# Moving one more block of w2 to the upper column groups in the closing matmuls of a decode layer

## The chip, the cores and the metric

The kernel runs on 1 core of one Trainium2 chip. The metric is the device time of one execution in microseconds; medians of several executions are quoted. A run's profile starts at the first instruction of the program and spans some 1.8 us less than the measured time. Times below that are given to a nanosecond (79.188 us) are read from the trace's records of single instructions and of semaphore updates, counted from the start of the span. Each trace is one execution.

The engines are named as in the profile: PE multiplies matrices and PEld loads its weights, DVE is the vector engine, ACT the scalar engine, and SyncE (SP, with its queue SPq) issues the transfers. The granted clock is the share of full speed that PE was allowed. ffn1 and ffn2 are the first and the second matrix product of the feed-forward part.

Ratios are the mean time of one kernel's fast runs over that of the other's fast runs of the same rounds, so they are not quite the ratios of the medians quoted beside them.

## The reference

One decode step of an adaptive layer: a modulation from `c`, windowed attention over a key and value cache, and a ReLU feed-forward part. The argument is about the last lines:

```python
mod = (_silu(c) @ w_mod).reshape(c.shape[0], 6, 1, -1)
sa, ca, ga, sb, cb, gb = ...
...
h = _layernorm(x) * (1 + cb) + sb
x = x + gb * (relu(h @ w1) @ w2)      # batch 4, 512 -> 1792 -> 512
```

w1 and w2 are 1792 KB each; with the cache window, wq, wo and w_mod the kernel reads 32 MB.

## The kernel before

One queue streams every weight in a fixed order; w1 and w2 come last, w2 in five pieces. A block is 128 of the 1792 hidden features, so w2 has 14 blocks (`FT` = 14).

```python
nc.sync.dma_start(out=w1_sb, in_=B_w1.rearrange("(p t) n -> p t n", t=DT))
W2_CHUNKS = [(0, 4), (4, 4), (8, 3), (11, 2), (13, 1)]      # first block, number of blocks
for (m0, e) in W2_CHUNKS:
    nc.sync.dma_start(out=w2_dst[:, m0 * D:(m0 + e) * D],
                      in_=B_w2[m0 * P:(m0 + e) * P, :].rearrange("(q e) n -> q (e n)", e=e))
```

The second matrix product uses 32 columns of the array per matmul. Four such column groups exist. A block in the lower groups (0 and 1) sums into `z_ps`, one in the upper groups (2 and 3) into `za_ps`; a block is four matmuls, two steps (`x`) of two groups (`g`). "Lone" below means that only two of the four groups work in a step.

```python
def closing(parts):
    for x in range(NX):                       # NX = 2
        for (ps, q, j, src, rhs, start, stop, cols) in parts:
            for g in range(2):
                q0 = (q + g) * CG             # CG = 32
                nc.tensor.matmul(out=ps[q0:q0 + CG, cols], lhsT=rows(src, j, x), rhs=rhs(2 * x + g),
                                 start=start and x == 0, stop=stop and x == NX - 1, tile_position=(0, q0))
...
ZUP = (0, 1, 2, 3, 6, 7)
ZLOW = tuple(m for m in range(FT) if m not in ZUP)
...
def zpart(m):
    mine = ZUP if m in ZUP else ZLOW
    return (za_ps if m in ZUP else z_ps, 2 if m in ZUP else 0, m, uT32, lambda j: w2_sb[:, m, j * DH2:(j + 1) * DH2],
            m == mine[0], m == mine[-1], slice(None))

for (m0, m1) in [(0, 8), (8, FT)]:
    ffn1(m0, m1)
for ms in [(0,), (1,), (2, 4), (3, 5), (6,), (7,)]:
    closing([zpart(m) for m in ms])
zc = work.tile([2 * CG, DH2], f32, name="zc")
nc.scalar.copy(out=zc[:], in_=za_ps[2 * CG:P, :])                       # ACT
nc.vector.tensor_tensor(out=zc[:], in0=zc[:], in1=gb2[:], op=ALU.mult)  # DVE
nc.vector.tensor_tensor(out=zc[:], in0=zc[:], in1=x12_ps[:], op=ALU.add)
for m in range(8, FT):
    closing([zpart(m)])
zg = work.tile([2 * CG, DH2], f32, name="zg")
nc.vector.tensor_tensor(out=zg[:], in0=z_ps[:], in1=gb2[:], op=ALU.mult)
res = work.tile([2 * CG, DH2], bf16, name="res")
nc.vector.tensor_tensor(out=res[:], in0=zg[:], in1=zc[:], op=ALU.add)
... # two DMAs store res
```

Of the kernel before, what the change touches and what calls it, by code (L numbers as in the profile page):

```python
# [17 lines left out]
def kernel(  # L18
# [23 lines left out]
    FT = Dff // P  # L42
# [146 lines left out]
    def closing(parts):  # L189
        for x in range(NX):  # L190
            for (ps, q, j, src, rhs, start, stop, cols) in parts:
                for g in range(2):
                    q0 = (q + g) * CG
                    nc.tensor.matmul(out=ps[q0:q0 + CG, cols], lhsT=rows(src, j, x), rhs=rhs(2 * x + g),  # L194
                                     start=start and x == 0, stop=stop and x == NX - 1, tile_position=(0, q0))
# [272 lines left out]
        return w1_sb[:, t, m0 * P + m - m0:(m0 + e) * P:e]  # L468


    ZUP = (0, 1, 2, 3, 6, 7)
    ZLOW = tuple(m for m in range(FT) if m not in ZUP)
    z_ps = psA.tile([2 * CG, DH2], f32, tag="t", name="z_ps")
    za_ps = psA.tile([P, DH2], f32, tag="t", name="za_ps")

    def ffn1(m0, m1):
        u_ps = psA.tile([P, m1 - m0, 2, B], f32, tag="t", name=f"u_ps_{m0}")
        for m in range(m0, m1):
            for t in range(DT):
                nc.tensor.matmul(out=u_ps[:, m - m0].rearrange("p s b -> p (s b)"), lhsT=w1_cols(t, m),  # L480
                                 rhs=ab[:, t].rearrange("p s b -> p (s b)"), start=(t == 0), stop=(t == DT - 1))
        us = work.tile([P, m1 - m0, B], f32, name=f"us_{m0}")
        nc.vector.tensor_tensor(out=us[:], in0=u_ps[:, :, 0, :], in1=rstd2[:].unsqueeze(1).to_broadcast([P, m1 - m0, B]),
                                op=ALU.mult)
        nc.vector.tensor_tensor(out=us[:], in0=us[:], in1=u_ps[:, :, 1, :], op=ALU.add)
        nc.vector.tensor_scalar_max(out=put(uT32[:, m0:m1, :]), in0=us[:], scalar1=0.0)
# [5 lines that stand above are left out]

    for (m0, m1) in [(0, 8), (8, FT)]:
        ffn1(m0, m1)
    for ms in [(0,), (1,), (2, 4), (3, 5), (6,), (7,)]:
        closing([zpart(m) for m in ms])
    zc = work.tile([2 * CG, DH2], f32, name="zc")
    nc.scalar.copy(out=zc[:], in_=za_ps[2 * CG:P, :])
    nc.vector.tensor_tensor(out=zc[:], in0=zc[:], in1=gb2[:], op=ALU.mult)
    nc.vector.tensor_tensor(out=zc[:], in0=zc[:], in1=x12_ps[:], op=ALU.add)  # L500
    for m in range(8, FT):
        closing([zpart(m)])

    zg = work.tile([2 * CG, DH2], f32, name="zg")
# [36 lines left out]
```

## Time and profile before

| | before |
|---|---|
| median of 3 runs (range) | 85.43 us (85.37 to 85.53) |
| span of the profile | 83.66 us |
| last landing of w1 | 75.70 us |
| last landing of w2 blocks 8-10 / 11-12 / 13 | 79.188 / 79.828 / 80.152 us |
| first matmul of block 8 / 11 | 79.229 / 79.869 us |
| DVE starts zg | 80.731 us |

A landing is the last of the increments that a transfer gives its semaphore. The lines of the profile behind the table, and how they are read, stand in the prediction.

### The profile page before, as it was taken

How to read it: one execution, taken by the hardware profiler on the slowest of the kernel's cores; microseconds unless marked ns; L12 is line 12 of the kernel's file. 1: busy time of each engine (PE TensorE's matmuls, PEld its weight loads, DVE VectorE, ACT ScalarE, POOL GpSimd, SP SyncE). 2: the span in 40 equal slices, each digit the busy share in tenths (PEclk: the TensorE clock that was granted, in tenths of full speed). 3: DMA queues.
4: the chain of work that ended last, by engine and by line, in shares of the span. 5: the costliest groups of instructions: out<-in, count | busy, mean ns of one | idle time of the engine just before them, and what ended most of it. 6: DMA issues, size and time to landing. Idle time of an engine off the chain costs nothing.

```text
span 83.7 us, 2373 instructions
## 1 busy us (share of the span) xinstructions
PE 56.1 (67%) x1064; PEld 47.0 (56%) x1064; DVE 26.5 (32%) x76; ACT 23.8 (28%) x38; POOL 6.0 (7%) x21
## 2 busy tenths in 40 slices
PE   0001006999953989999999905999555779577950
PEld 0000006995852964988777504999555248567740
DVE  0201300367043010375546668650003120251350
ACT  3201001664302000697777819611000010001000
POOL 5894000000000000000000000000000000000000
PEclk9999999999985555799999998589555555555555
DMA  2899999998999999999999999999999999999600
GB/s 31 306 466 423 407 427 423 529 501 360 392 380 423 419 423 415 415 427 419 415 419 423 423 415 419 419 427 419 415 415 431 407 415 436 426 388 403 251 8 2
DMA packets 4257, 32.14 MB, mean 384 GB/s; under 512 B 528, under 2 KB 664, under 8 KB 1304
## 3 DMA queue, kind: packets, MB, share of 16 engines
q1 hardware_dynamic: 4192, 31.99, 92.2%
q8 instruction: 8, 0.13, 0.6%
q10 hardware_dynamic: 24, 0.01, 0.0%
q0 software_dynamic: 32, 0.00, 0.0%
q14 instruction: 1, 0.01, 0.0%
HBM read 31.99 MB, written 0.00 MB: 382 GB/s over the span
## 4 chain that ended last, share of the span: by engine, by line
DMA 63%; PE 27%; DVE 4%; issue 1%; SPq 1%; ACT 1%; DVEq 0%
DMA w<-in_B_w_dram 26%; DMA v<-in_A_v_cache_dram 24%; DMA k<-in_A_k_cache_dram 14%; PE ktp L225 9%; PE qT_ps L322 4%; PE sc_ps L237 2%; PE z_ps L194 2%; PE mT L273 2%; PE mT L275 2%; PE u_ps L480 1%; PE za_ps L194 1%; PE m_ps L259 1%; PE m_ps L262 1%; PE st_ps_var L289 1%; PE gb_ps L194 1%
## 5 line engine op out<-in xcount | busy, mean ns | idle before, releaser
L225 PE MATMUL ktp<-ident_k,k 128*128 128x128 bf16 x256 | 18.2, 240 | 5.6 <-DMA k<-in_A_k_cache_dram 5.6
L225 PEld LDWEIGHTS <-k 128*128 128x128 bf16 x256 | 17.2, 110 | 8.2 <-DMA k<-in_A_k_cache_dram 5.7
L230 ACT COPY kT<-ktp 128x1024 bf16<-128x1024 bf16 x16 | 15.5, 1015 | 17.4 <-PE ktp L225 16.3
L228 DVE COPY kT<-ktp 128x1024 bf16<-128x1024 bf16 x16 | 11.1, 692 | 16.2 <-PE ktp L225 15.9
L360 PE MATMUL oT_ps<-pT,v 128*128 128x16 bf16 x256 | 7.1, 172 | 1.9 <-issue 1.9
L360 PEld LDWEIGHTS <-v 128*128 128x128 bf16 x256 | 7.1, 100 | 2.0 <-issue 2.0
L237 PE MATMUL sc_ps<-kT,qpad 128*32 128x512 bf16 x64 | 5.6, 445 | 0.4 <-DVE qpad L326 0.4
L377 PE MATMUL pT_ps<-ident_bf,p_rep 128*128 128x128 bf16 x32 | 3.3, 291 | 2.9 <-DVE p_rep L371 2.9
L200 PE MATMUL tp<-ident_bf,cx_sb 8*128 8x8 bf16 x4 | 0.3, 174 | 7.3 <-POOL xs L180 7.3
L377 PEld LDWEIGHTS <-p_rep 128*128 128x128 bf16 x32 | 2.9, 135 | 3.4 <-DVE p_rep L371 3.4
L322 PE MATMUL qT_ps<-hT,wq_sb 128*128 128x4 bf16 x128 | 3.6, 166 | 1.4 <-DVE ab L315 1.4
L322 PEld LDWEIGHTS <-wq_sb 128*128 128x128 bf16 x128 | 3.5, 104 | 1.5 <-DMA wq_sb<-in_A_wq_dram 1.5
L200 PEld LDWEIGHTS <-cx_sb 8*128 8x128 bf16 x4 | 0.2, 114 | 7.3 <-DMA cx_sb<-in_A_x_dram 7.3
L429 ACT COPY y<-y_ps 128x256 f32<-128x256 f32 x1 | 0.4, 372 | 9.6 <-DVE y L428 9.6
L424 PE MATMUL y_ps<-wo_sb,o 128*32 128x512 bf16 x16 | 2.1, 619 | 1.0 <-DVE o L415 0.9
L436 PEld LDWEIGHTS <-wo_sb 128*128 128x128 bf16 x64 | 2.5, 120 | 0.6 <-DMA wo_sb<-in_A_wo_dram 0.6
L402 DVE TENSOR_TENSOR oT_sb<-oT_ps,rb 128x128 bf16<-128x128 f32 x1 | 0.3, 291 | 7.8 <-PE oT_ps L360 7.8
L436 PE MATMUL y_ps<-o,wo_sb 128*128 128x4 bf16 x64 | 2.4, 173 | 0.5 <-DMA wo_sb<-in_A_wo_dram 0.5
L371 DVE TENSOR_TENSOR p_rep<-e_sb,mi 128x512 int32<-128x512 int32 x4 | 2.5, 686 | 0.7 <-ACT e_sb L366 0.7
L194 PEld LDWEIGHTS <-uT 128*32 128x32 bf16 x56 | 2.3, 135 | 0.6 <-issue 0.2
L432 PEld LDWEIGHTS y_ps<-sel_b,y 128*128 128x128 f32 x8 | 1.8, 327 | 1.4 <-DVE y L428 1.4
L237 PEld LDWEIGHTS <-qpad 128*32 128x32 bf16 x64 | 1.3, 103 | 2.2 <-DVE qpad L326 0.7
(113 smaller groups left out, 56.2 us busy)
## 6 DMA issues: line engine op xcount, KB each, us to landing
k<-in_A_k_cache_dram SPq DMA_DIRECT2D x8, 1024.0 KB, 28.4
v<-in_A_v_cache_dram SPq DMA_DIRECT2D x8, 1024.0 KB, 19.8
wq_sb<-in_A_wq_dram SPq DMA_DIRECT2D x1, 4096.0 KB, 23.6
wo_sb<-in_A_wo_dram SPq DMA_DIRECT2D x4, 1024.0 KB, 19.9
wmod_sb<-in_w_mod_dram SPq DMA_DIRECT2D x1, 2304.0 KB, 9.5
w<-in_B_w_dram SPq DMA_DIRECT2D x1, 1792.0 KB
w<-in_B_w_dram SPq DMA_DIRECT2D x2, 512.0 KB, 19.9
wmod_sb<-in_w_mod_dram SPq DMA_DIRECT2D x1, 768.0 KB, 4.4
```

Of the source, the lines that this page charges most:

```text
L194: nc.tensor.matmul(out=ps[q0:q0 + CG, cols], lhsT=rows(src, j, x), rhs=rhs(2 * x + g), start=start and x == 0, stop=stop and x == NX - 1, ...
L225: nc.tensor.transpose(out=tp[:, ii, :], in_=k_tiles[gi][:, iq * IQ + ii, :], identity=ident_k)
L228: nc.vector.tensor_copy(out=dst, in_=tp[:])
L230: nc.scalar.copy(out=dst, in_=tp[:])
L237: nc.tensor.matmul(out=sc_ps[hw * CG:(hw + 1) * CG, half * HALF:(half + 1) * HALF], lhsT=qpad[:, b, par, hw, :], rhs=kT[:, half * (NI // 2 ...
L322: nc.tensor.matmul(out=qT_v[:, hq, :], lhsT=wq_sb[:, t, hq * Dh:(hq + 1) * Dh], rhs=hT[:, t, :], start=(t == 0 and hq == 0), stop=(t == DT ...
L360: nc.tensor.matmul(out=oT_ps[:, hw, par].rearrange("p b r -> p (b r)"), lhsT=v_tiles[h][:, i, :], rhs=pT[:, i, c0:c0 + B * rep], start=(fi ...
L371: nc.vector.tensor_tensor(out=p_w[:, ws, :], in0=e_w[:, ws].unsqueeze(2).to_broadcast([P, WQ // 2, B]), in1=mi4[:].unsqueeze(1).to_broadca ...
L377: nc.tensor.transpose(out=tp[:, ii, :], in_=p_rep[:, i // 2, :, i % 2], identity=ident_bf[:])
L424: nc.tensor.matmul(out=y4_ps[q0:q0 + CG, :], lhsT=o4[:, l, g % 2, g // 2, :], rhs=wo_sb[:, g, l, :], start=(g == 0 and l < 4), stop=(g == ...
L432: nc.tensor.matmul(out=y_ps[:, t, :], lhsT=y4[:, t, :], rhs=sel_b[:], start=(t == 0), stop=False)
L436: nc.tensor.matmul(out=y_ps[:, m, :], lhsT=wo_sb[:, g, l, m::DT], rhs=o4[:, l, g % 2, g // 2, 0:B], start=False, stop=(g == NP - 1 and l = ...
```

## The change

Its intent is to shorten the run of lone steps at the end: block 8 goes to the upper groups and is issued beside block 9, so that the four matmuls of a step work in four column groups.

```diff
-    ZUP = (0, 1, 2, 3, 6, 7)
+    ZUP = (0, 1, 2, 3, 6, 7, 8)
...
-    for ms in [(0,), (1,), (2, 4), (3, 5), (6,), (7,)]:
+    for ms in [(0,), (1,), (2, 4), (3, 5), (6,), (7,), (8, 9)]:
         closing([zpart(m) for m in ms])
...
-    for m in range(8, FT):
+    for m in range(10, FT):
         closing([zpart(m)])
```

## The prediction

> **What bounds the kernel now.** I started with the page, to see which resource is busy where. Its DMA rows, and the table of transfers by size, are:
>
> ```profile
> DMA  2899999998999999999999999999999999999600
> GB/s 31 306 466 423 407 427 423 529 501 360 392 380 423 419 423 415 415 427 419 415 419 423 423 415 419 419 427 419 415 415 431 407 415 436 426 388 403 251 8 2
> ...
> w<-in_B_w_dram SPq DMA_DIRECT2D x1, 384.0 KB, 17.7
> ...
> w<-in_B_w_dram SPq DMA_DIRECT2D x1, 256.0 KB, 15.9
> w<-in_B_w_dram SPq DMA_DIRECT2D x1, 128.0 KB, 13.7
> ```
>
> One slice is 83.7/40 = 2.09 us. From slice 2 to slice 37 (to 77.4 us) the 16 DMA engines are nine tenths busy at 400 to 430 GB/s, and slice 38 (77.4 to 79.5 us) still moves 251 GB/s. So the stream of weights reaches into the stage that the change touches: w2 comes in five pieces, and the three lines are its last three: blocks 8 to 10 (384 KB), 11 and 12 (256 KB), 13 (128 KB). The last number is the time from issue to landing. The issues stand in the SyncE rows of the timeline; each line is the answer for its own short window, in the order of the pieces:
>
> ```profile
> 61.46 0.33 SPq L129 DMA_DIRECT2D w<-in_B_w_dram  x1
> ...
> 63.95 0.33 SPq L129 DMA_DIRECT2D w<-in_B_w_dram  x1
> ...
> 66.44 0.33 SPq L129 DMA_DIRECT2D w<-in_B_w_dram  x1
> ```
>
> The sums give the landings: 61.46 + 17.7 = 79.16, 63.95 + 15.9 = 79.85, 66.44 + 13.7 = 80.14 us. The trace's records of the semaphore updates have them finer: blocks 8 to 10 at 79.188, 11 and 12 at 79.828, 13 at 80.152 us; blocks 4 to 7 at 78.258.
>
> Next I read the chain that ended last, because it should name what sets the end:
>
> ```profile
> 53.99 21.72 DMA w<-in_B_w_dram
> ...
> 78.91 0.34 PE za_ps L194 x8
> 79.25 1.46 PE z_ps L194 x24
> 80.71 0.02 issue
> 80.73 0.29 DVE zg L505
> ```
>
> Taken alone it says that 24 lone z_ps matmuls (blocks 8 to 13, four each) stand on the path for 1.46 us, and that DMA left the path when w1 landed at 75.70. I don't believe the second part. The timeline of the tail shows why:
>
> ```profile
> 78.62 0.64 PE L194 MATMUL za_ps<-w,uT 128*32 128x128 bf16 x8
> 79.23 1.46 PE L194 MATMUL z_ps<-w,uT 128*32 128x128 bf16 x24
> 79.23 1.19 PEld L194 LDWEIGHTS <-uT 128*32 128x32 bf16 x23 [0.25 <-issue]
> 79.29 0.26 ACT L498 COPY zc<-za_ps 64x128 f32<-64x128 f32 x1 [3.58 <-PE za_ps L194]
> 79.59 0.28 DVE L499 TENSOR_TENSOR zc<-zc,gb 64x128 f32<-64x128 f32 x1 [1.29 <-ACT zc L498]
> 79.91 0.28 DVE L500 TENSOR_TENSOR zc<-zc,x_ps 64x128 f32<-64x128 f32 x1
> 80.73 0.28 DVE L505 TENSOR_TENSOR zg<-z_ps,gb 64x128 f32<-64x128 f32 x1 [0.55 <-PE z_ps L194]
> ```
>
> The weight loads are idle for 0.25 us before 79.23, put down to "issue", that is, to nothing the profile could name. Matmul by matmul, the starts in the trace fill this in. A pair of block 7 starts at 78.937 and 78.938; the next could follow 0.107 us later, at 79.045, yet block 8 starts at 79.229. That is 0.041 us after its piece of w2 landed (79.188). Block 11 starts at 79.869, again 0.041 us after its piece (79.828). Block 4 starts at 78.302, 0.044 us after its piece (78.258), although there a free slot falls on the same moment. So PE follows the stream of w2 with almost no work in hand, and the chain view misses these waits. Blocks 8 to 10 end their last slot at 79.739 + 0.107 = 79.846, only 0.023 us before block 11 can start. From 79.869 on, three blocks run back to back (last start 80.379, end 80.693), and zg follows at 80.731.
>
> **What the Trainium skill says.** "TensorE: Matmul & The Clock Gate", section Back-to-back issue gap, gives N/1.2 ns per matmul at the cold clock, 106.7 ns for N = 128. The trace agrees: the granted clock in the tail is 0.50 and starts in one column group are 106 to 107 ns apart. The same page, Part 3: Packing small matmuls, says that matmuls in different column tiles run concurrently; in the paired steps of blocks 2, 4 and 3, 5 the four matmuls of a step start within 0.021 us, and steps follow every 0.107 us, as they do for two matmuls alone. Perfetto Trace Analysis, Roofline, puts a single core's ceiling at some 435 GB/s over 16 DMA engines; the rows above run at 400 to 430. "DMA: Bandwidth & Descriptors", section Why a DMA increments its semaphore by 16 and not by 1, says that only the full count means the data has landed. I therefore took the last of the increments as each piece's landing, and the 0.041 us starts agree.
>
> **The change, part by part.** No instruction is added or removed: 56 matmuls, 56 weight loads, and the same ACT and DVE operations. Block 8's four matmuls move from z_ps (column groups 0 and 1) to za_ps (groups 2 and 3), and are issued interleaved with block 9's.
>
> On PE: blocks 8 and 9 one after the other take 4 steps, together 2. The saving is 2 steps x 0.107 = 0.214 us of PE time. Where it falls: the pair needs the piece of blocks 8 to 10, as block 8 does now, so it starts at 79.229 again. Before, six steps filled 79.229 to 79.846 (0.617 us). Four steps end at 79.846 - 0.214 = 79.632 us. Block 11 still needs its piece, landed at 79.828, and starts at 79.869. PE's wait before it grows from 0.023 to 79.869 - 79.632 = 0.237 us. Blocks 11 to 13 are unchanged, so the last z_ps matmul ends at 80.693 and zg starts at 80.731, as now. Gain at the end: 0.
>
> On ACT and DVE: the sum in za_ps is now complete with block 8 instead of block 7. Its last matmul is that of the pair's second step. In the first paired step of before, z_ps starts at 78.302 and the second step's za_ps at 78.405, so 0.103 us later: 79.229 + 0.103 = 79.332, and with 0.314 us duration the end is 79.646 us (before 78.938 + 0.314 = 79.252). The ACT copy followed by 0.041 us: 79.687. The copy's start to the end of the second zc operation took 79.907 + 0.279 - 79.293 = 0.893 us before. So zc is ready at about 80.58 us, and DVE can take zg 0.035 us later, at 80.615. It needs it at 80.731. The slack shrinks from 80.731 - (80.186 + 0.035) = 0.510 us to 0.116 us, and stays positive: cost 0.
>
> DMA: nothing in the diff changes an issue or what an issue waits for. Sum: 0.00 us, so 85.43 stays 85.43; I round to 85.4.
>
> **Rivals.** First, the change works as intended, and the time falls by the whole 0.214 us to 85.43 - 0.21 = 85.2. For it: the chain view shows z_ps matmuls on the path and no DMA after 75.70. Against it: the two starts, each 0.041 us after a landing, with 0.640 us between the landings and 0.640 between the starts. It would need the 256 KB piece to land some 0.2 us nearer to the 384 KB one, and the stream's rate leaves no room: 256 KB (262,144 bytes) in 0.640 us is 410 GB/s, the rate of the whole stream.
>
> Second, the later za_ps makes zc the last to arrive, and DVE takes zg late. The slack of 0.116 us would have to be overdrawn, by a slower copy or by one more wait on PE. If za_ps came another 0.2 us late, zg would start 0.08 us late and the time would be 85.5. For it: the slack left is less than half a DVE operation (0.283 us), and the copy and the two zc operations now hang on block 8's late piece. Against it: each term of the 0.116 us comes from a row of the same trace, and all three operations keep their size.
>
> Third, a mixture: PE's idle 0.2 us could move the granted clock. The clock is 0.50 throughout the tail already, after stretches at full speed, and the idle time is short; I give it nothing.
>
> **Range and chances.** Every mechanism lies between -0.21 and +0.1 us, that is -0.25% to +0.1%. The three runs of before spread by 0.16 us, and another chip or build may shift the median by as much again. I take 85.15 to 85.7 as the range for 8 in 10. Two per cent are 1.7 us, eight times the largest effect that I can name: faster 0.01, same 0.98, slower 0.01.
>
> **What would show it right or wrong.** Right: the first z_ps and za_ps matmuls of blocks 8 and 9 start together at the landing of the 384 KB piece plus 0.04 us; block 10 ends 0.2 us or more before the 256 KB piece lands; block 11 starts 0.04 us after that landing, with PE idle before it; the copy of za_ps starts near 79.69 instead of 79.29; DVE's idle time before zg shrinks from 0.55 to about 0.15 us, still ended by z_ps. Wrong: block 11 starts as soon as block 10 has ended, earlier than now relative to the end of the stream (first rival), or zg follows zc within 0.04 us (second rival). A larger move would mean that w2's landings themselves moved, which no line of the diff explains.

## The result

The changed kernel takes 85.50 us (median of 6 runs, 85.36 to 85.72), the kernel before in the same rounds 85.43 us (85.37 to 85.67). The ratio is 1.0005, with a 95% interval of 0.9987 to 1.0023: the same. A gain of the whole 0.214 us of the prediction's first rival would be a ratio of 0.9975, which lies outside the interval.

These are the three last pieces of w2 in the DMA view of the changed kernel (size, median time from issue to landing):

```profile
w<-in_B_w_dram SPq DMA_DIRECT2D x1, 384.0 KB, 17.9
...
w<-in_B_w_dram SPq DMA_DIRECT2D x1, 256.0 KB, 16.0
w<-in_B_w_dram SPq DMA_DIRECT2D x1, 128.0 KB, 13.9
```

They are issued at 61.49, 63.98 and 66.45 us. Issues and times to landing are those of before to within 0.2 us, so the transfers were not touched. Now the timeline of its tail (start, duration, engine, line, operation, tiles, count, idle time and what ended it):

```profile
79.40 0.29 PE L194 MATMUL z_ps<-w,uT 128*32 128x128 bf16 x2
79.45 0.34 PE L194 MATMUL za_ps<-w,uT 128*32 128x128 bf16 x2
79.48 1.38 PE L194 MATMUL z_ps<-w,uT 128*32 128x128 bf16 x18
79.82 0.26 ACT L498 COPY zc<-za_ps 64x128 f32<-64x128 f32 x1 [3.94 <-PE za_ps L194]
80.03 0.55 PEld L194 LDWEIGHTS <-uT 128*32 128x32 bf16 x11 [0.19 <-issue]
80.12 0.28 DVE L499 TENSOR_TENSOR zc<-zc,gb 64x128 f32<-64x128 f32 x1 [1.67 <-ACT zc L498]
80.44 0.28 DVE L500 TENSOR_TENSOR zc<-zc,x_ps 64x128 f32<-64x128 f32 x1
80.89 0.28 DVE L505 TENSOR_TENSOR zg<-z_ps,gb 64x128 f32<-64x128 f32 x1 [0.17 <-PE z_ps L194]
```

The reader should look at three rows. The za_ps and z_ps rows at 79.40 to 79.48 are blocks 8 and 9, which now run side by side. The weight loads (PEld) are idle for 0.19 us before 80.03, "issue" again: that is block 11, and the idle time was not there before. And DVE's idle time before zg is 0.17 us where it was 0.55, still ended by z_ps.

The chain that ended last (start, duration) shows the same place:

```profile
54.05 21.82 DMA w<-in_B_w_dram
...
79.79 0.22 PE z_ps L194 x5
80.01 0.02 issue
80.03 0.84 PE z_ps L194 x12
...
80.89 0.29 DVE zg L505
```

In its terms nothing is amiss: records of PE run to 80.01, and 0.02 us of "issue" follow. It names neither landing, because a matmul's record lasts 0.31 us and covers the gap.

Single starts and landings give the account to the nanosecond. The last three pieces of w2 landed 0.160 to 0.166 us later in this profile than in that of before (w1 too, 75.87 against 75.70; in unpaired_a below, which has the same transfers, the last piece lands at 80.150 as before), so the last column takes 0.160 off.

| us | before | changed | difference, less 0.160 |
|---|---|---|---|
| blocks 8-10 landed | 79.188 | 79.348 | 0 |
| first matmul of block 8 | 79.229 | 79.391 | 0.002 |
| last step of block 10 starts | 79.739 | 79.693 | -0.206 |
| blocks 11-12 landed | 79.828 | 79.988 | 0 |
| first matmul of block 11 | 79.869 | 80.030 | 0.001 |
| ACT copy of za_ps starts | 79.293 | 79.824 | 0.371 |
| second zc operation starts | 79.907 | 80.438 | 0.371 |
| zg starts | 80.731 | 80.892 | 0.001 |

The two steps are saved on PE (-0.206 us). PE then stands still: block 10's last step occupies its groups until 79.693 + 0.107 = 79.800, and block 11 starts at 80.030, so the wait is 0.230 us where it was 0.023.

### The profile page after: what moved, and what is told of

The parts are those of the page before. It is cut to its first block, busy times and chain, and to the rows that moved or that the text cites. A ratio compares the mean times of both kernels' runs of the same rounds, so it can differ in the third digit from the quotient of the medians.

```text
span 83.8 us, 2373 instructions
## 1 busy us (share of the span) xinstructions
PE 56.8 (68%) x1064; PEld 47.3 (56%) x1064; DVE 26.5 (32%) x76; ACT 23.9 (28%) x38; POOL 5.9 (7%) x21
## 4 chain that ended last, share of the span: by engine, by line
DMA 78%; PE 14%; SPq 2%; DVE 2%; issue 1%; DVEq 0%
DMA wq_sb<-in_A_wq_dram 28%; DMA w<-in_B_w_dram 26%; DMA v<-in_A_v_cache_dram 23%; PE qT_ps L322 4%; PE sc_ps L237 2%; PE ktp L225 2%; PE za_ps L194 2%; PE z_ps L194 2%; SPq L83 2%; PE u_ps L480 1%; SPq L93 0%; SPq L92 0%; DVE zg L505 0%; DVE res L507 0%; DVE qpad L326 0%
## 5 line engine op out<-in xcount | busy, mean ns | idle before, releaser
L225 PE MATMUL ktp<-ident_k,k 128*128 128x128 bf16 x256 | 18.7, 243 | 5.6 <-DMA k<-in_A_k_cache_dram 5.6
L377 PE MATMUL pT_ps<-ident_bf,p_rep 128*128 128x128 bf16 x32 | 2.8, 244 | 2.9 <-DVE p_rep L371 2.9
L377 PEld LDWEIGHTS <-p_rep 128*128 128x128 bf16 x32 | 2.1, 109 | 3.6 <-DVE p_rep L371 3.5
```

The source lines that it names most:

```text
L225: nc.tensor.transpose(out=tp[:, ii, :], in_=k_tiles[gi][:, iq * IQ + ii, :], identity=ident_k)
L377: nc.tensor.transpose(out=tp[:, ii, :], in_=p_rep[:, i // 2, :, i % 2], identity=ident_bf[:])
```

## The experiments

The theory: PE waits for the pieces of w2, and this wait swallows the saved steps (landing theory). The main rivals: the gap before block 8 is something else; pairing saves nothing; zc has become the last. Twelve kernels were run in three sessions: noland_b, noland_a, merge_b and merge_a; then, on another chip, the fills and up12; then the rest. The kernel before took 85.68, 85.60 and 85.65 us in them (medians of 11 runs each). Since profiles differ by up to 0.4 us in when the stream ends, the traces are compared from a landing, or from the first ffn2 matmul, to zg.

**noland_b and noland_a: blocks 8 to 13 of w2 are not read.** Both give wrong results, the first from the kernel before, the second from the changed one. All pieces are still loaded, and blocks 4 to 7 still wait for theirs.

```diff
-  lambda j: w2_sb[:, m, j * DH2:(j + 1) * DH2]
+  lambda j: w2_sb[:, m % 8, j * DH2:(j + 1) * DH2]
```

> The kernel before, but the matmuls of blocks 8 to 13 multiply by blocks 0 to 5 of w2, which landed early (wrong result on purpose); all pieces are still loaded. Landing theory (PE waits for the pieces of w2, and that hid the change): block 8 follows block 7 without the gap, 0.107 us after it, all twelve lone steps run back to back, and zg starts 0.155 us earlier relative to the first ffn2 matmul, ratio about 0.998. Rival (the gap before block 8 is something else, such as a fixed cost of turning to the other accumulator): the gap of 0.18 us stays and the ratio is 1.000.

> The changed kernel with the same edit (wrong result on purpose). Landing theory: with the waits gone the two saved steps count, z_ps is complete 0.214 us sooner than in noland_b; but zc, ready about 0.07 us later than that, becomes the last, so zg starts about 0.145 us sooner than in noland_b and 0.30 us sooner than in the kernel before: ratio about 0.9965, and DVE takes zg 0.035 us after zc. Rival (a paired step costs as much as two lone ones): no difference from noland_b.

noland_b: 85.11 us, ratio 0.9936 (0.9915 to 0.9956). noland_a: 85.30 us, ratio 0.9957 (0.9938 to 0.9975). The gap before block 8 is gone, so it was the landing. But the size is off: zg starts 2.441 us after the first ffn2 matmul instead of 2.944, that is 0.50 us sooner and not 0.155. The timeline of noland_b tells why:

```profile
78.88 0.32 PE L194 MATMUL za_ps<-w,uT 128*32 128x128 bf16 x2
78.96 0.32 PE L194 MATMUL z_ps<-w,uT 128*32 128x128 bf16 x2
78.98 0.32 PE L194 MATMUL za_ps<-w,uT 128*32 128x128 bf16 x2
...
79.20 0.32 PE L194 MATMUL za_ps<-w,uT 128*32 128x128 bf16 x2
79.28 1.17 PE L194 MATMUL z_ps<-w,uT 128*32 128x128 bf16 x18
...
80.49 0.28 DVE L505 TENSOR_TENSOR zg<-z_ps,gb 64x128 f32<-64x128 f32 x1
```

Before the z_ps row at 78.96, z_ps had eight matmuls, those of blocks 4 and 5; so this row is block 8. It starts while za_ps has the second step of block 6 and both steps of block 7 still to come (78.98 to 79.20), although these six matmuls stand ahead of it in the program, whose order on every engine is that of the kernel before. Here PE let a matmul go whose column groups were free; how far ahead it can reach was not measured. So steps of the lower and the upper groups need not be issued side by side to run so, and "lone" steps add up only where a landing holds them. Only the landing of blocks 4 to 7 at 78.511 still holds z_ps: it starts at 78.554 and runs without a break to its last start at 80.134, 16 steps, one every 0.105 us.

noland_a was to be 0.145 us sooner than noland_b and is 0.10 us later (2.540 us from the first ffn2 matmul to zg); the means of the timed runs, 85.31 and 85.13, go the same way. Its timeline:

```profile
79.39 0.74 PE L194 MATMUL z_ps<-w,uT 128*32 128x128 bf16 x10
...
80.27 0.28 DVE L500 TENSOR_TENSOR zc<-zc,x_ps 64x128 f32<-64x128 f32 x1
80.48 0.27 DVE L505 TENSOR_TENSOR zg<-z_ps,gb 64x128 f32<-64x128 f32 x1
```

The z_ps row ends at 80.13 (its last step starts at 79.823), yet zg starts at 80.476, 0.206 us after the second zc operation and with no wait of its own: it queued behind zc. Hence:

**nozc_a: noland_a with less work on zc.**

```diff
-    nc.vector.tensor_tensor(out=zc[:], in0=zc[:], in1=gb2[:], op=ALU.mult)
```

> noland_a without the multiplication of zc by gb2 (wrong on purpose), so zc is ready 0.32 us sooner. If zc was what held noland_a back, zg now follows z_ps: about 2.24 us after the first ffn2 matmul instead of 2.54, ratio to the kernel before about 0.992, and the change's two steps show at last: 0.2 us less than noland_b's 2.44. Rival (something else on PE holds noland_a): zg stays at 2.5 us.

85.04 us, ratio 0.9929 (0.9907 to 0.9951). Its output is wrong, which doesn't matter for the time. From the first ffn2 matmul to zg it takes 2.240 us, as expected, 0.201 us less than noland_b.

```profile
79.55 0.74 PE L194 MATMUL z_ps<-w,uT 128*32 128x128 bf16 x10
...
80.33 0.28 DVE L504 TENSOR_TENSOR zg<-z_ps,gb 64x128 f32<-64x128 f32 x1
```

z_ps ends at 80.29 and zg follows 0.04 us later. Counted from the landing of blocks 4 to 7, which z_ps waits for in both kernels, zg comes after 1.764 us here and 1.978 in noland_b: 0.214 us less. So the two steps are worth 0.2 us, and in the changed kernel two things in a row stand before them: the landings, and zc behind those. The timed ratios of nozc_a and noland_b, from different sessions, are too close to show it; the traces do.

**merge_b and merge_a: one landing instead of two.** The same bytes, correct results. `W2_CHUNKS` also sets the stride at which ffn1 reads the columns of w1 (`w1_cols`): its matmuls for blocks 8 to 12 start 0.040 us apart instead of 0.026 to 0.030. That does not reach the end, since `uT` is complete at 78.65 us in merge_b and 78.89 in merge_a, long before the merged piece lands (79.887 and 80.124).

```diff
-    W2_CHUNKS = [(0, 4), (4, 4), (8, 3), (11, 2), (13, 1)]
+    W2_CHUNKS = [(0, 4), (4, 4), (8, 5), (13, 1)]
```

> The kernel before with blocks 8 to 12 of w2 in one piece of 640 KB instead of 384 and 256. Landing theory: block 8 now starts 0.04 us after the merged piece lands, near where block 11 started, and twelve steps in a row follow: zg 0.64 us later, ratio about 1.0075. Rival (landings do not set the tail): ratio 1.000.

> The changed kernel with the same merged piece. Landing theory: no landing falls after the pair any more, so the saved steps count up to where zc takes over: zg 0.12 us sooner than in merge_b, 0.52 us later than in the kernel before, ratio about 1.006, zg 0.035 us after zc. Rival (pairing saves nothing): the same as merge_b.

merge_b: 86.16 us, ratio 1.0064 (1.0041 to 1.0088). merge_a: 86.06 us, ratio 1.0046 (1.0026 to 1.0065). In merge_b the wait is long enough for the profile to name it:

```profile
79.93 1.46 PE L194 MATMUL z_ps<-w,uT 128*32 128x128 bf16 x24 [0.55 <-DMA w<-in_B_w_dram]
```

It is the wait before the same block 8 that the profile of before called "issue". After it twelve steps run in a row, and zg comes 1.543 us after the merged landing. In merge_a it is 1.345 us: the pair gains 0.198 us once no later landing stands behind it. The means of the timed runs, 86.22 and 86.07, agree in sign and size, though their intervals overlap. I had expected a gain of 0.12 us only, with zc taking over:

```profile
80.17 0.29 PE L194 MATMUL za_ps<-w,uT 128*32 128x128 bf16 x2 [0.54 <-DMA w<-in_B_w_dram]
...
81.21 0.28 DVE L500 TENSOR_TENSOR zc<-zc,x_ps 64x128 f32<-64x128 f32 x1
81.47 0.28 DVE L505 TENSOR_TENSOR zg<-z_ps,gb 64x128 f32<-64x128 f32 x1
```

zg does not read zc; only res does. DVE starts it as early as 0.206 us after the second zc operation started (noland_a), not 0.28 + 0.035 us. In merge_a that allows 81.212 + 0.206 = 81.418, and z_ps was the later one.

**after_fill2, before_fill2 and after_fill8: filling the hole.** Lone steps into a tile that nobody reads (`fill_ps`, of the size of `z_ps`), between blocks 10 and 11; n is 1 or 4, each turn being two steps. Results are correct.

```diff
     for m in range(10, FT):      # range(8, FT) in before_fill2
         closing([zpart(m)])
+        if m == 10:
+            for i in range(n):
+                closing([(fill_ps, 0, 9, uT32, lambda j: w2_sb[:, 9, j * DH2:(j + 1) * DH2], i == 0, i == n - 1, slice(None))])
```

> The changed kernel plus two lone steps (four matmuls of block 9 into a PSUM tile that nobody reads) between blocks 10 and 11. Landing theory: they fit the hole of 0.23 us before block 11; ratio to the kernel before 1.000, block 11 still 0.04 us after its piece. Rival (PE steps set the end): 0.21 us more, ratio 1.0025.

> The kernel before plus the same two lone steps in the same place. Landing theory: there is no hole there (0.023 us), so block 11 starts 0.19 us late and the end moves by as much, ratio 1.0022. Rival (PE time is free throughout the tail): 1.000.

> The changed kernel plus eight lone steps in the same place. Landing theory: 8 x 0.107 - 0.23 = 0.62 us late, ratio 1.0073. Rival (PE steps set the end already): 0.86 us, 1.010.

after_fill2: 85.71 us, ratio 1.0017 (1.0000 to 1.0033). before_fill2: 85.79 us, ratio 1.0023 (1.0004 to 1.0043). after_fill8: 86.17 us, ratio 1.0065 (1.0053 to 1.0078), which leaves the rival's 1.010 out. The two small fills cannot be told apart by their times. The trace of after_fill2 can be read:

```profile
79.82 0.43 PE L194 MATMUL fill_ps<-w,uT 128*32 128x128 bf16 x4
...
80.06 0.82 PE L194 MATMUL z_ps<-w,uT 128*32 128x128 bf16 x12
```

The fill's last step starts at 79.929 and the piece lands at 80.017; block 11 starts 0.042 us after that, and zg 0.905 us after it, where the kernel before has 0.903 and the changed one 0.904. The hole was free. With eight steps it is 1.554 us, that is 0.65 us more, against an expected 0.62. before_fill2 is a poor witness: in its profile the granted clock rose from 0.50 to 1.00 at 80.67 us, within the last steps, so zg came only 0.952 us after the landing; block 11, though, started at 80.285, 0.211 us after the landing instead of 0.041.

**up12: the late zc priced.** Block 12 instead of block 8 in the upper groups of the kernel before; correct result.

```diff
-    ZUP = (0, 1, 2, 3, 6, 7)
+    ZUP = (0, 1, 2, 3, 6, 7, 12)
-    for ms in [(0,), (1,), (2, 4), (3, 5), (6,), (7,)]:
+    for ms in [(0,), (1,), (2, 4), (3, 5), (6,), (7,), (8,), (9,), (10,), (11, 12)]:
...
-    for m in range(8, FT):
+    for m in range(13, FT):
```

> The kernel before with block 12, not block 8, moved to the upper groups and issued beside block 11; za_ps is then complete 0.64 us after the landing of blocks 8 to 10. This prices the late zc: z_ps could end 0.1 us sooner than before, but zc follows za_ps by 0.93 us, so zg starts 0.035 us after zc, about 0.52 us later than in the kernel before: ratio about 1.006. Rival (zc is hidden whatever za_ps does): 0.999 to 1.000.

86.05 us, ratio 1.0053 (1.0040 to 1.0066):

```profile
81.27 0.28 DVE L500 TENSOR_TENSOR zc<-zc,x_ps 64x128 f32<-64x128 f32 x1
81.47 0.28 DVE L505 TENSOR_TENSOR zg<-z_ps,gb 64x128 f32<-64x128 f32 x1
```

zc sets the end here: zg starts 1.311 us after the landing of blocks 11 and 12, 0.41 us later than in the kernel before (expected 0.52; the 0.11 too much is again the DVE overlap). The second rival of the prediction is real, then, only not in reach of the change.

**unpaired_a: the other column groups alone, without the issue side by side.**

```diff
-    for ms in [..., (6,), (7,), (8, 9)]:
+    for ms in [..., (6,), (7,), (8,), (9,)]:
```

> One part of the change alone: block 8 in the upper groups, but issued before block 9 and not interleaved with it. The runs without landings suggest that PE starts a matmul whose column group is free although an earlier one of another group still waits for its group. If so, block 9 starts within 0.02 us of block 8 as in the changed kernel, zg comes 0.90 us after the 256 KB piece landed, ratio 1.000. Rival (strict order): block 9 starts about 0.2 us after block 8; the end still doesn't move, since the hole before block 11 covers it.

85.51 us, ratio 0.9990 (0.9970 to 1.0010). The weight loads of block 8 begin when its piece has landed (79.181), and z_ps of block 9 follows at once:

```profile
79.22 0.46 PEld L194 LDWEIGHTS <-uT 128*32 128x32 bf16 x12 [0.16 <-issue]
79.24 0.29 PE L194 MATMUL z_ps<-w,uT 128*32 128x128 bf16 x2
79.28 0.34 PE L194 MATMUL za_ps<-w,uT 128*32 128x128 bf16 x2
```

Block 9 starts 0.013 us after block 8 (79.236 against 79.223), and zg 0.904 us after the 256 KB landing. The interleaved issue does nothing that PE does not do by itself.

**fine_b and fine_a: finer last pieces.** The runs above say that the only thing left to gain here is the work behind the last landing. Same bytes, correct results.

```diff
-    W2_CHUNKS = [(0, 4), (4, 4), (8, 3), (11, 2), (13, 1)]
+    W2_CHUNKS = [(0, 4), (4, 4), (8, 2), (10, 2), (12, 1), (13, 1)]
```

> The kernel before with finer last pieces of w2: blocks 8-9, 10-11, 12, 13 instead of 8-10, 11-12, 13; the same bytes. Landing theory: after the last landing only block 13 is left, so zg comes 0.48 us after it instead of 0.58: 0.10 us sooner, ratio 0.999 if the smaller pieces do not slow the stream. Rival (the smaller pieces cost more than that): ratio over 1.000.

> The changed kernel with the same finer pieces. Landing theory: PE has caught up before the last landing in either kernel, so it equals fine_b: zg 0.48 us after the last landing, ratio 0.999. Rival (the two saved steps add to it): 0.21 us below fine_b.

fine_b: 85.92 us, ratio 1.0035 (1.0008 to 1.0063). fine_a: 85.91 us, ratio 1.0031 (1.0006 to 1.0056). Up to zg both do what the theory says: 0.479 us after the last landing in either, against 0.579 in the kernel before. Nevertheless they are slower.

zg and the first store, at 80.65 and 81.28, are 0.08 us earlier than in the kernel before (80.73 and 81.36), and the second store has landed at 82.667 instead of 82.749. From there to the end of the span it takes 1.121 us instead of 0.908. At its end, SyncE waits for the semaphores of all transfers in a fixed order. In the kernel before the stores use the last two of them (numbers 117 and 118). One more transfer shifts the rotation: a store now uses number 107, which stands second in the order, so SyncE waits there until 82.69 and only then goes through the remaining four waits, some 0.06 us each. This accounts for the span of this profile (0.213 - 0.082 = 0.131 us longer: 83.788 against 83.657). It was not tested by itself, but merge_b and merge_a fit it: with one transfer fewer, their stores use numbers 116 and 117, one wait stands behind them, and the stretch is 0.967 and 0.956 us. The timed means of fine_b and the kernel before differ by more, 0.30 us (interval 0.07 to 0.54); the profiled execution was the fastest of the six. Whether the smaller pieces also slow the stream, as the rival has it, stays open. A version with finer last pieces but the old number of transfers, such as blocks 0-5, 6-9, 10-11, 12, 13, was not run. No kernel of this study with correct results beats both.

## Why the prediction was right

It gave 85.4 us, a range of 85.15 to 85.7 and 0.98 for "same"; 85.50 us came.

- **What bounds the tail.** PE waits for the landings of w2. Shown: the gap before block 8 vanishes when blocks 8 to 13 are not read, and where the wait is longer (merge_b) the profile itself puts it down to the transfer.
- **PE saves 0.214 us and waits as much longer before block 11.** Measured 0.206 saved, and a wait of 0.230 instead of the predicted 0.237 us. That this wait is free time is shown by after_fill2 (from landing to zg 0.905 us) and after_fill8.
- **zc stays hidden.** The copy was predicted 0.394 us later than before (79.687) and came 0.371 later. The slack before zg was sized as 0.116 us; by the same rule it is 80.892 - (80.718 + 0.035) = 0.139. The rule itself was too strict: zg need not wait for the end of the second zc operation, so the slack is 80.892 - (80.438 + 0.206) = 0.248 us. That is a term mis-sized on the safe side.
- **First rival, 0.214 us of gain.** Its size was right and its place wrong. It appears where no landing stands behind the pair: 0.198 us in merge_a against merge_b, 0.201 in nozc_a against noland_b.
- **Second rival, zc last.** It did not happen in the changed kernel; it does in up12 and noland_a.
- **Third rival.** The granted clock was 0.50 throughout the tail of the changed kernel too.
- **A loose reading.** The prediction puts the stream at 400 to 430 GB/s from slice 2 to 37, but its own row has 306 to 529 up to slice 12 (and 388 to 436 after it). With each packet's bytes spread over its duration, every stretch of 2 us between 4 and 76 us moves 411 to 434 GB/s, so what follows from it stands.

One sentence of the working holds only by circumstance: that blocks 8 and 9 "one after the other take 4 steps". They do because the landing comes after block 7 has ended. Without it PE runs block 8 beside blocks 6 and 7 unasked, and so my expectations for noland_b and noland_a missed, the second even in sign.

## What to carry to other kernels

Where a stream of weights ends inside the last stage, compare each group's first start with the landing of what it reads before counting instructions; work saved ahead of a landing is only a longer wait. The chain of waits can hide such a landing when matmul records are longer than the gap. And when a change moves work to a side sum, ask how much later that sum's own chain of operations ends, since it may be the next bound.

## What the Trainium skill lacked or had wrong

- "TensorE: Matmul & The Clock Gate", Part 3: Packing small matmuls, says that matmuls keep program order in start and end. In noland_b block 8's first z_ps matmul starts at 78.956 us, before the second step of block 6 and both steps of block 7 in za_ps (78.982 to 79.196), which precede it in the program; in unpaired_a a matmul of block 9 starts at 79.240, before two of block 8 at 79.284 and 79.306.
- No page that I read tells of the closing waits at the program's end and their order: one more transfer in fine_b made the stretch from the last landing of a store to the end of the span 1.121 us instead of 0.908.
- No page that I read says how far apart the 16 DMA engines can end: in the profile of before, eight increments of the last piece came from 78.42 to 78.81 us and the other eight from 79.34 to 80.15. Why was not studied.
